# Planning an attention, Fourier-mix and MLP kernel with longer store and load latencies, and mirrored DFT tiles placed behind the last direct one

## The chip, the cores and the metric

The kernel runs on one core of one Trainium2 chip. The metric is device time in microseconds; for the kernel before it is 289.15 us, the median of 3 runs (288.5 to 289.49). The profile that is read below is one execution of it, with a span of 287.8 us from the first to the last instruction.

Short names used for the engines: PE is TensorE's matmuls, PEld its weight loads, DVE is VectorE, ACT is ScalarE, POOL is GpSimd, SP is the sync engine. SPq and POOLq are the instruction queues of SP and POOL, where DMA transfers are issued.

## The reference

Two computations follow each other, with 4 batches, 8 heads, 768 positions, 64 elements per head and a model width of 512:

```python
def _attn_ref(q, k, v, sort_net):
    ...
    P = sort_net                                   # 8 x 8 per head, five Sinkhorn steps
    ...
    k_sorted = np.einsum('bhij,bhjcd->bhicd', P, k_b)
    v_sorted = np.einsum('bhij,bhjcd->bhicd', P, v_b)
    scores = scale * np.matmul(q_b, k_sb.transpose(0, 1, 2, 4, 3))   # within blocks of 96
    ...                                            # softmax
    return np.matmul(attn, v_sb).reshape(B, H, S, D)

def _moe_ref(x, w_ch1, w_ch2):
    X = np.fft.fft(np.fft.fft(x, axis=1), axis=2)
    u = x + np.real(X)
    un = (u - mean(u)) / np.sqrt(var(u) + 1e-06)   # over the model width
    return u + np.maximum(un @ w_ch1, 0.0) @ w_ch2 # 512 -> 2048 -> 512
```

## The kernel before

**Work per batch.** For each of the 4 batches `b`, the kernel mixes keys and values with the Sinkhorn matrix (`kqt` L927 for keys, `v_mix` L742 for values, the latter fed by copies into `vcx` at L726), computes block scores (`scores`, L982), their exponentials on ACT (L991) with a correction by -1 (L1004 on DVE, L1006 on ACT), and the product with the values (`av`, L1021; then a reciprocal L1033 and a scaling L1036 on DVE). The result of a batch lies in a tile `rt`.

The Fourier mix has two stages. `dft1` transforms along the sequence: DVE folds `rt` (L1053 to L1137), PE multiplies (L1093 to L1103), ACT writes `y`. `dft2(b, g)` transforms along the model width. It works on 6 token tiles of 128 rows in two halves: `g = 0` has the tiles `T` = 0, 1, 2, `g = 1` has 3, 4, 5. Tiles 0, 1, 2 and 5 are direct: four matmuls of 256 columns with `y` (L1179) and one of 512 with the row terms `rb` (L1183), in a PSUM bank. Tiles 3 and 4 are mirrored: they reuse the banks of tiles 0 and 1, add one matmul (L1168), and are read backwards. For every tile DVE adds the residue into a buffer `u` (L1190 direct, L1202 and L1211 for `g = 1`), takes the statistics (L1216, L1218), and after ACT has computed the inverse deviation (L1222, L1225) the normalised rows `un` are written (L1242 on DVE, L1238 on ACT) and transposed into `ut` (by PE for batch 0, by SP's transposing DMA L1249 for the others).

`mlp(b, g)` takes `ut` of 384 tokens through both layers: 64 matmuls of the first layer (L1278, into banks of the group `pm`), 16 ReLU evictions into `hr` (L1290 on ACT, L1287 on DVE), 48 matmuls of the second layer (L1299), and per tile one DVE addition into `u` (L1307). Each tile of `u` is then stored: those of `g = 0` by SP as plain DMAs (L1312; the third tile in three pieces, L1314, L1316 and L1318, of 112, 15 and 1 rows), called the direct stores, and those of `g = 1` by POOL as an indirect DMA over a list of rows (L1322).

**Buffers that tie these together.** There are 6 buffers `u`, so `u` of `dft2(b+1, 0)` can only be written once the direct store of the same tile of batch `b` has landed. There are 5 PSUM banks in the group `pf` (scores, products, DFT) and 3 in `pm` (MLP). The transposed queries `qt` have 3 buffers. The keys and queries of batches 2 and 3 are loaded by POOL (`load_qk`, L500), and their transfers are held back by `after=lns[1:2]` until a certain normalisation of batch 0; these are the gated loads. Queries of batches 2 and 3 are transposed by SP (L945).

**The order.** A planner in the kernel (`Plan`) sets the order of all instructions before the program is built. Each operation is added with a pair of figures per engine, the time for which the engine is occupied and the time until the result can be used, and with a priority (`at(...)` sets it for a group, lower is sooner). `schedule` plays this forward: at each step the engine that is free first takes the operation of lowest priority figure that is ready, and buffers come free at the planned end of their last user. The planned times are used for nothing but the order; on the chip, each engine runs its list in that order and waits on semaphores for real. A planned figure that is too short thus places an instruction too early in its engine's list, and everything behind it on that engine then waits with it.

The change and the prediction's steps touch: `load` (L472, with `o.late` at L477), `dft2` (L1146, the mirrored branch L1164 to L1171, the direct one L1172 to L1187), the store in `mlp` (L1331), and the priorities of `dft2` at L1368, L1374 and L1377.

Of the kernel before, what the change touches and what calls it, by code (L numbers as in the profile page):

```python
# [348 lines left out]
def mm(n, k=1):  # L349
    return k * (n / 2400.0 + 0.004)  # L350


def pe(t):
    return {"PE": (t, t + 0.17)}
# [12 lines left out]
def kernel(  # L367
# [20 lines left out]
    P = Plan()  # L388
# [83 lines left out]
    def load(dst, src, nbytes, w, prio, eng="POOL", r=(), after=()):  # L472
        e = {"POOL": nc.gpsimd, "SP": nc.sync}[eng]
        c = (0.8, 0.8) if eng == "POOL" else (0.1, 2.3)
        o = P.add({eng: c}, lambda _: e.dma_start(dst, src), r=r, w=w,  # L475
                  prio=prio, nbytes=nbytes, tag="load", after=after)
        o.late = 4.0 if after else 0.0  # L477
        return o

    spin = Buf("pm")  # L480
# [1 line left out]
          tag="spin")  # L482
# [56 lines left out]
    for n in range(2):  # L539
# [10 lines left out]
          w=["smalls"], prio=-4996.6, tag="small")  # L550
# [53 lines left out]
    for it in range(5):  # L604
# [27 lines left out]
        r=["phi"], w=["pk"] + hk(1), tag="pk")  # L632
    P.add({"DVE": (0.14, 0.21)}, lambda _: V.tensor_tensor(
        phl[1], pw, phl[0], op=ALU.subtract), r=["pw", "phi"],
        w=["plo"] + hk(1), tag="pk", prio=P.prio + 20)
    for n, d_ in enumerate((pvh, pvl)):
# [5 lines left out]
              r=[("phi", "plo")[n]], w=[("pvh", "pvl")[n]] + hk(1), tag="pv",  # L642
# [8 lines left out]
    for hh in range(2):  # L651
        def f(_, hh=hh):
# [12 lines left out]
          r=[bk], w=["tkh"], prio=8.0, tag="tkh")  # L665
# [476 lines left out]
        chain(3)  # L1142

    banks_of = {}

    def dft2(b, g):  # L1146
        rt = rts[b]
# [3 lines left out]
        ym = [(y, c) for c in range(4)]  # L1151
        lts = [("rb", n) for n in range(4)] + [
            "rrow", "lt", "lt96", "lt96a", "lt96b", "lt96c", "dtab"]
        if g == 1:
            P.add({"DVE": (0.08, 0.16), "ACT": (0.18, 0.23)}, lambda e: copy(
                e, y.ap[:, :, 383:384], y.ap[:, :, 385:386]),
                r=ym, w=[(y, "z")] + ym, tag="yz")
        for tt in range(3):
            T = 3 * g + tt
            u, st = Buf("u"), Buf("st")  # L1160
            us[b, g].append(u)
            w0 = 128 * (T if T < 3 else 2)
            l0 = 128 * T if T < 3 else 384
            if T in (3, 4):  # L1164
                ps = banks_of[b, T - 3]

                def f(_, ps=ps, T=T):
                    nc.tensor.matmul(  # L1168
                        ps.ap, lt[:, LTD + 128 * (T - 3):LTD + 128 * (T - 2)],
                        rb, start=False, stop=True, skip_group_check=True)  # L1170
                P.add(pe(mm(512) + 0.03), f, r=lts, w=[ps, u], tag="dft2")  # L1171
            else:  # L1172
                ps = Buf("pf")
                banks_of[b, T] = ps

                def f(_, ps=ps, w0=w0, l0=l0):
                    for c in range(4):
                        o = 256 * (c % 2)
                        nc.tensor.matmul(  # L1179
                            ps.ap[:, o:o + 256], y.ap[:, c, w0:w0 + 128],  # L1180
                            dtab[:, c, :], start=(c == 0), stop=False,
                            skip_group_check=True)
                    nc.tensor.matmul(ps.ap, lt[:, l0:l0 + 128], rb,  # L1183
                                     start=False, stop=True,
                                     skip_group_check=True)
                P.add(pe(mm(256, 4) + mm(512) + 0.05), f,
                      r=ym + lts, w=[ps, u], tag="dft2")  # L1187
            if T < 3:
                P.add({"DVE": (0.6, 0.69)}, lambda _, u=u, ps=ps, T=T:
                      V.scalar_tensor_tensor(  # L1190
                          u.ap.rearrange("p (m n) -> p m n", n=2),
                          rt.ap[:, T, :].rearrange("p (m n) -> p m n", n=2),
                          RSC, ps.ap.rearrange("p (n m) -> p m n", n=2),
                          op0=ALU.mult, op1=ALU.add),
                      r=[ps] + [(rt, h) for h in range(H)], w=[u], tag="u")
            else:
                def f(_, u=u, ps=ps, T=T):
                    p_ = ps.ap
                    rev = bass.AP(
                        tensor=p_.tensor, offset=p_[:, 511:512].offset,  # L1200
                        ap=[p_.ap[0], [-1, 255], [-256, 2]])
                    V.scalar_tensor_tensor(  # L1202
                        u.ap[:, 1:511].rearrange("p (m n) -> p m n", n=2),
                        rt.ap[:, T, 1:511].rearrange(
                            "p (m n) -> p m n", n=2),
                        RSC, rev, op0=ALU.mult, op1=ALU.add)
                P.add({"DVE": (0.6, 0.69)}, f,
                      r=[ps] + [(rt, h) for h in range(H)], w=[u], tag="u")

                def f(_, u=u, ps=ps, T=T):  # L1210
                    V.scalar_tensor_tensor(  # L1211
                        u.ap[:, 0:512:511], rt.ap[:, T, 0:512:511], RSC,
                        ps.ap[:, 0:512:256], op0=ALU.mult, op1=ALU.add)
                P.add({"DVE": (0.1, 0.18)}, f,
                      r=[ps] + [(rt, h) for h in range(H)], w=[u], tag="u")
            P.add({"DVE": (0.6, 0.69)}, lambda _, u=u, st=st: V.bn_stats(  # L1216
                st.ap, u.ap), r=[u], w=[st], tag="bn")
            P.add({"DVE": (0.1, 0.17)}, lambda _, tt=tt, st=st: V.bn_aggr(  # L1218
                mv.ap[:, tt, :], st.ap), r=[st], w=[(mv, tt)], tag="bna")
# [4 lines left out]
            w=[(ny, 0)], tag="ln")  # L1224
# [4 lines left out]
            r=mvs + [ny], w=[nm], tag="ln")  # L1229
# [3 lines left out]
        for tt in range(3):  # L1233
            un, pt, u = Buf("un"), Buf("pf"), us[b, g][tt]

            def f(e, tt=tt, un=un, u=u):
# [4 lines left out]
                else:  # L1241
# [4 lines left out]
                  r=[u, ny, nm] + mvs, w=[un], tag="un")  # L1246
            if b > 0:
# [3 lines left out]
                      r=[un], w=[(ut, tt, 1)], tag="uX")  # L1251
                continue

            def f(_, un=un, pt=pt):
                p16 = pt.ap.bitcast(F16)
                for c in range(4):
# [10 lines left out]
                  r=[pt], w=[(ut, tt, 1)], tag="utev")  # L1267
# [3 lines left out]
    def mlp(b, g, pr_pe, pr_v):  # L1271
        ut = uts[b, g]
        for fc in range(16):
            ps = Buf("pm")

            def f(_, fc=fc, ps=ps):
                for c in range(4):
# [5 lines left out]
                  tag="ff1")  # L1283

            def f(e, fc=fc, ps=ps):
# [3 lines left out]
                else:  # L1289
# [3 lines left out]
                  w=[("h", g, fc)], prio=pr_v, tag="relu")  # L1293
        for tt in range(3):
            ps, u = Buf("pm"), us[b, g][tt]
            for qd in range(4):
                def f(_, qd=qd, tt=tt, ps=ps):
                    for fc in range(4 * qd, 4 * qd + 4):
# [4 lines left out]
                      r=[("w2", qd)] + [  # L1303
                          ("h", g, fc) for fc in range(4 * qd, 4 * qd + 4)],
                      w=[ps], prio=pr_pe + 0.1, tag="ff2")
# [3 lines left out]
            def f(_, u=u, T=3 * g + tt):  # L1309
# [16 lines left out]
                for x in st_:  # L1326
# [1 line left out]
                        tc.declare_no_dep(x.ins, y.ins,   # L1328
                                          reason="each row stored once")
                (stores if T > 2 else direct).extend(st_)  # L1330
            P.add({"SP": (0.1, 2.3)} if g == 0 else {"POOL": (1.2, 3.5)}, f,  # L1331
                  r=[(u, 1), "rows"], w=[], prio=pr_v, tag="out")


# [11 lines left out]
    def at(p, *fns):  # L1346
        for fn, a in fns:
            P.prio = p
            fn(*a)
# [15 lines left out]
    for hf in range(2):  # L1365
        load_qk("k", 2, hf, 62.0 + hf)
        load_qk("q", 2, hf, 62.5 + hf)
    at(20.0, (dft1, (1,)), (dft2, (1, 0)), (dft2, (1, 1)))  # L1368
    at(14.0, (a_path, (1,)), (a_rows, (2,)))
    at(30.0, (make_bdk, (2,)), (attn, (2,)))  # L1370
    for hf in range(2):
        load_qk("k", 3, hf, 64.0 + hf)
        load_qk("q", 3, hf, 64.5 + hf)
    at(40.0, (dft1, (2,)), (dft2, (2, 0)), (dft2, (2, 1)))  # L1374
    at(35.0, (a_rows, (3,)))
    at(50.0, (make_bdk, (3,)), (attn, (3,)))
    at(55.0, (dft1, (3,)), (dft2, (3, 0)), (dft2, (3, 1)))  # L1377
    for b in range(B):
        for g in range(2):
            mlp(b, g, 100.0 + 10 * (2 * b + (g if b < B - 1 else 1 - g)),  # L1380
# [43 lines left out]
```

## Time and profile before

| stretch, us | what runs mostly | PE busy, us | DVE busy, us | granted PE clock |
|---|---|---|---|---|
| 20 to 40 | attention of batch 0 | 18.90 of 20 | 18.97 | 1.00 |
| 40 to 60 | attention of batch 1, first Fourier mix | 18.60 of 20 | 19.71 | 1.00 |
| 60 to 80 | end of attention 1, MLP (0, 0) begins | 19.14 of 20 | 19.92 | 1.00 |
| 80 to 100 | values for batches 2 and 3, MLP (0, 0) | 19.50 of 20 | 19.43 | 1.00 |
| 100 to 120 | dft2 (1, 0), attention of batch 2, MLP (0, 1) | 16.03 of 20 | 13.90 | 0.91 |
| 120 to 280 | the rest, mostly MLP | 159.86 of 160 | 66.39 | 1.00 |

How to read it: busy time is the share in which an engine executes an instruction of the program; [...]. The stores and loads that the change speaks of take, from issue to landing: plain direct stores of 256 KB 2.0 us in the median and 4.1 us at most, the 15-row pieces 1.9, 4.7 and 7.5 us (smallest, median, largest), the indirect stores 2.7 us in the median, the gated loads that still run after 60 us between 4.9 and 9.8 us.

### The profile page before, as it was taken

How to read it: one execution, taken by the hardware profiler on the slowest of the kernel's cores; microseconds unless marked ns; L12 is line 12 of the kernel's file. 1: busy time of each engine (PE TensorE's matmuls, PEld its weight loads, DVE VectorE, ACT ScalarE, POOL GpSimd, SP SyncE). 2: the span in 40 equal slices, each digit the busy share in tenths (PEclk: the TensorE clock that was granted, in tenths of full speed). 3: DMA queues.
4: the chain of work that ended last, by engine and by line, in shares of the span. 5: the costliest groups of instructions: out<-in, count | busy, mean ns of one | idle time of the engine just before them, and what ended most of it. 6: DMA issues, size and time to landing. Idle time of an engine off the chain costs nothing.

```text
span 287.8 us, 5930 instructions
## 1 busy us (share of the span) xinstructions
PE 270.7 (94%) x2355; PEld 157.0 (55%) x2355; DVE 172.1 (60%) x424; ACT 158.0 (55%) x332; POOL 55.0 (19%) x81
## 2 busy tenths in 40 slices
PE   5999998999999986999999999999999999999991
PEld 2558876555745553554567456445545545545540
DVE  4599999999999974773489654136214415410010
ACT  2589889759689343885378126416704614614600
POOL 8993304150000280001300000021000012000022
PEclk9999999999999999799999999999999999999998
DMA  7999999999010299222102011211121012022002
GB/s 113 218 257 245 214 208 211 220 185 160 9 24 7 44 182 134 60 53 64 69 19 57 0 75 38 56 75 46 41 92 39 20 35 109 21 61 77 10 17 92
DMA packets 42529, 26.33 MB, mean 91 GB/s; under 512 B 30106, under 2 KB 38824, under 8 KB 42500
## 3 DMA queue, kind: packets, MB, share of 16 engines
q0 software_dynamic: 23536, 18.31, 37.7%
q1 hardware_dynamic: 18966, 7.64, 12.1%
q8 instruction: 18, 0.29, 0.4%
q14 instruction: 9, 0.07, 0.1%
HBM read 28.96 MB, written 6.29 MB: 122 GB/s over the span
## 4 chain that ended last, share of the span: by engine, by line
issue 49%; PE 26%; DVE 15%; POOL 4%; DMA 3%; ACT 0%; POOLq 0%; SPq 0%; DVEq 0%
PE bank L1299 5%; PE bank L1278 5%; PE bank L1391 4%; POOL out_dram L1322 4%; DMA out_dram<-u 3%; PE bank L742 2%; DVE rt L1036 2%; PE bank L927 2%; DVE st L1216 1%; PE bank L982 1%; PE bank L745 1%; DVE eb L1004 1%; PE bank L1093 1%; DVE hr L1287 1%; DVE pmt L1053 1%
## 5 line engine op out<-in xcount | busy, mean ns | idle before, releaser
L1290 ACT ACTIVATE hr<-bank 128x384 f16<-128x384 f32 x106 | 52.0, 491 | 81.9 <-PE bank L1278 75.6
L1278 PE MATMUL bank<-ut,w1sb 128*128 128x384 f16 x512 | 94.3, 329 | 0.7 <-DVE hr L1287 0.4
L1299 PE MATMUL bank<-w2sb,hr 128*128 128x512 f16 x384 | 88.5, 379 | 0.0
L1278 PEld LDWEIGHTS <-w1sb 128*128 128x128 f16 x512 | 48.5, 98 | 34.8 <-issue 2.1
L1299 PEld LDWEIGHTS <-hr 128*128 128x128 f16 x384 | 36.7, 98 | 41.3
L1307 DVE TENSOR_TENSOR u<-bank,u 128x512 f32<-128x512 f32 x24 | 16.5, 689 | 58.5 <-PE bank L1299 58.5
L1322 POOL DMA_INDIRECT out_dram<-u,rows x12 | 11.7, 971 | 164.3 <-DVE u L1307 137.5
L991 ACT ACTIVATE ex<-bank 96x384 f32<-96x384 f32 x64 | 28.1, 484 | 1.6 <-PE bank L982 1.2
L1391 PE MATMUL bank<-pack 128*128 128x480 f16 x63 | 18.0, 419 | 3.3 <-DMA pack<-k_pack 3.3
L1190 DVE SCALAR_TENSOR_TENSOR u<-rt,bank 128x512 f32<-128x512 f16 x12 | 8.1, 684 | 18.6 <-PE bank L1183 13.6
L1202 DVE SCALAR_TENSOR_TENSOR u<-rt,bank 128x510 f32<-128x510 f16 x12 | 8.1, 676 | 18.5 <-PE bank L1168 9.5
L1021 PEld LDWEIGHTS <-eb 97*128 97x128 f16 x416 | 15.8, 98 | 4.1 <-issue 1.8
L1006 ACT ACTIVATE eb<-ex,negone 96x384 f16<-96x384 f32 x30 | 17.9, 615 | 0.2
L1021 PE MATMUL bank<-vsf,eb 97*128 97x65 f16 x416 | 16.9, 193 | 0.9 <-DVE un L815 0.4
L475 POOL DMA_DIRECT2D kq<-in_k_dram x8 | 8.0, 995 | 50.5 <-DVE vcx L726 33.9
L1036 DVE TENSOR_TENSOR rt<-bank,rz 128x384 f16<-128x384 f32 x32 | 17.2, 546 | 0.3
L475 POOL DMA_DIRECT2D kq<-in_q_dram x20 | 16.3, 833 | 2.8 <-DVE rz L1033 1.3
L678 ACT CAST vsf<-bank 96x512 f16<-96x512 f32 x19 | 13.9, 793 | 4.6 <-PE bank L742 4.5
L1216 DVE BATCH_NORM_STATS2 st<-u 128x6 f32<-128x512 f32 x24 | 16.1, 685 | 0.3
L982 PE MATMUL bank<-qt,ks 64*128 64x96 f16 x256 | 11.7, 207 | 2.9 <-DVE u L1190 2.5
L1287 DVE TENSOR_SCALAR hr<-bank 128x384 f16<-128x384 f32 x22 | 12.1, 548 | 2.5 <-PE bank L1278 2.3
L1238 ACT ACTIVATE un<-u,nm,ny 128x512 f16<-128x512 f32 x14 | 11.3, 808 | 3.5 <-DMA ut<-un 1.8
(131 smaller groups left out, 330.3 us busy)
## 6 DMA issues: line engine op xcount, KB each, us to landing
kq<-in_k_dram POOLq DMA_DIRECT2D x8, 384.0 KB, 12.5
w1sb<-in_moe_w_ch_dram POOLq DMA_DIRECT2D x4, 512.0 KB, 16.7
w2sb<-in_moe_w_ch_dram POOLq DMA_DIRECT2D x4, 512.0 KB, 19.5
out_dram<-u SPq DMA_DIRECT2D x8, 256.0 KB, 2.0
kq<-in_q_dram POOLq DMA_DIRECT2D x4, 384.0 KB, 8.1
hr<-in_v_dram POOLq DMA_DIRECT2D x2, 768.0 KB, 12.4
kq<-in_v_dram POOLq DMA_DIRECT2D x2, 768.0 KB, 21.2
kq<-in_q_dram POOLq DMA_DIRECT2D x16, 96.0 KB, 8.2
```

Source lines behind the costliest of these rows:

```text
L475: o = P.add({eng: c}, lambda _: e.dma_start(dst, src), r=r, w=w, prio=prio, nbytes=nbytes, tag="load", after=after)
L991: nc.scalar.activation(ex.ap, pss[h2].ap[0:96, 0:384], AF.Exp, scale=SCALE),
L1006: nc.scalar.activation(ed, src, AF.Identity, bias=negone[0:96])
L1021: nc.tensor.matmul(po.ap[:, 65 * T:65 * T + 65], eb.ap[:, e0:e0 + 128], vsf[:, vi:vi + 65], start=(n == 0), stop=(n == len(WIN[T]) - 1), s ...
L1036: P.add({"DVE": (0.45, 0.56)}, lambda _: V.tensor_tensor(rt.ap[:, :, D * h:D * h + D], po3()[:, :, 0:D], rz.ap[:, :, None].broadcast_to([1 ...
L1216: P.add({"DVE": (0.6, 0.69)}, lambda _, u=u, st=st: V.bn_stats(st.ap, u.ap), r=[u], w=[st], tag="bn")
L1278: nc.tensor.matmul(ps.ap[:, 0:GT], w1sb[:, c, 128 * fc:128 * fc + 128], ut.ap[:, c, :], start=(c == 0), stop=(c == 3))
L1290: nc.scalar.activation(hr[g][:, fc, :], ps.ap[:, 0:GT], AF.Relu)
L1299: nc.tensor.matmul(ps.ap, hr[g][:, fc, 128 * tt:128 * tt + 128], w2sb[:, fc, :], start=(fc == 0), stop=(fc == 15))
L1307: V.tensor_tensor(u.ap, ps.ap, u.ap, op=ALU.add),
L1322: st_ = [nc.gpsimd.indirect_dma_start(out.rearrange("b s m -> (b s) m"), bass.IndirectOffsetOnAxis(ap=rows[:, i:i + 1], axis=0), u.ap, None)]
L1391: nc.tensor.matmul(spin.ap[:, 0:480], idh, pack.bitcast(F16))
```

## The change

It changes what the planner assumes and two orders that it is given; no part of the computation is added or removed. One more warm-up matmul (L1391) is issued, 64 for 63, and some operations that either engine can do change hands between DVE and ACT: four ReLUs, two of the corrections by -1 and one PSUM copy go to ACT, two normalisations to DVE.

- The planned latency of a gated load grows from 4.0 to 6.0 us on top of the transfer.
- The planned latency of a direct store grows from 2.3 us to 7.0 us for batches 0 to 2 and to 2.6 us for batch 3. In the plan, a buffer `u` of `g = 0` is therefore free later, and the DVE instruction that writes it next is placed later in DVE's list.
- The mirrored tiles 3 and 4 are planned only behind the last direct tile of `g = 0` (an order for PE, not a dependency of data).
- For batches 1 to 3, `dft2(b, 1)` gets a priority figure that is 0.5 higher than that of `dft2(b, 0)`, so that it follows it.

```diff
-        o.late = 4.0 if after else 0.0
+        o.late = 6.0 if after else 0.0
...
     banks_of = {}
+    d2last = []
...
-                P.add(pe(mm(512) + 0.03), f, r=lts, w=[ps, u], tag="dft2")
+                P.add(pe(mm(512) + 0.03), f, r=lts, w=[ps, u], tag="dft2",
+                      after=[d2last[-1]])
...
-                P.add(pe(mm(256, 4) + mm(512) + 0.05), f,
-                      r=ym + lts, w=[ps, u], tag="dft2")
+                d2last.append(P.add(
+                    pe(mm(256, 4) + mm(512) + 0.05), f,
+                    r=ym + lts, w=[ps, u], tag="dft2"))
...
-            P.add({"SP": (0.1, 2.3)} if g == 0 else {"POOL": (1.2, 3.5)}, f,
+            P.add({"SP": (0.1, 7.0 if b < 3 else 2.6)} if g == 0 else {"POOL": (1.2, 3.5)}, f,
...
-    at(20.0, (dft1, (1,)), (dft2, (1, 0)), (dft2, (1, 1)))
+    at(20.0, (dft1, (1,)), (dft2, (1, 0)))
+    at(20.5, (dft2, (1, 1)))
...
-    at(40.0, (dft1, (2,)), (dft2, (2, 0)), (dft2, (2, 1)))
+    at(40.0, (dft1, (2,)), (dft2, (2, 0)))
+    at(40.5, (dft2, (2, 1)))
...
-    at(55.0, (dft1, (3,)), (dft2, (3, 0)), (dft2, (3, 1)))
+    at(55.0, (dft1, (3,)), (dft2, (3, 0)))
+    at(55.5, (dft2, (3, 1)))
```

## The prediction

> **What bounds the kernel now.** I read the busy line of the page first, then PE's busy time and clock by stretches of the span, then what PE waited for, and last the timelines around the one stretch that stood out.
>
> ```profile
> PE 270.7 (94%) x2355; PEld 157.0 (55%) x2355; DVE 172.1 (60%) x424; ACT 158.0 (55%) x332; POOL 55.0 (19%) x81
> ...
> 70.00:100.00 30.00, 29.36 (x284) 17.41 (x283) 29.35 (x58) 21.28 (x47) 1.33 (x2) 1.00 0.16 30
> 100.00:120.00 20.00, 16.03 (x177) 9.93 (x176) 13.90 (x35) 9.62 (x22) 6.87 (x10) 0.91 1.25 132
> 120.00:282.00 162.00, 161.86 (x1092) 87.56 (x1088) 66.39 (x154) 73.52 (x160) 11.95 (x22) 1.00 0.18 50
> ```
>
> PE is the bound. The columns after the length of a stretch are PE, PEld, DVE, ACT, POOL, then the granted clock. From 120 us to the last matmul PE has no gap (161.86 of 162), so every microsecond won or lost before 120 us reaches the end. Between 100 and 120 us PE idles 4.0 us and the clock falls to 0.91. The stretch in slices of 2 us shows where:
>
> ```profile
> 112.00:114.00 2.00, 0.55 (x10) 0.40 (x10) 1.28 (x3) 0.00 (x0) 0.00 (x0) 1.00 1.34 104
> 114.00:116.00 2.00, 1.57 (x8) 0.61 (x6) 2.00 (x6) 0.95 (x4) 0.00 (x0) 0.66 0.64 105
> 116.00:118.00 2.00, 2.00 (x14) 0.88 (x13) 1.58 (x5) 1.68 (x6) 0.00 (x0) 0.50 0.05 11
> ```
>
> PE stands still and then works at half clock for a while. The next fence puts together lines of PE's timeline (three), DVE's (one), and the chain of waits (one); each has start, length, and what.
>
> ```profile
> 107.85 0.60 PE L1179 MATMUL bank<-vcx,y 128*128 128x256 f16 x4 [1.09 <-DVE rt L1036]
> 113.45 0.35 PE L982 MATMUL bank<-qt,ks 64*128 64x96 f16 x8 [2.45 <-DVE u L1190]
> 114.98 1.44 PE L1278 MATMUL bank<-ut,w1sb 128*128 128x384 f16 x4 [0.43 <-DVE hr L1287]
> ...
> 112.72 0.69 DVE L1190 SCALAR_TENSOR_TENSOR u<-rt,bank 128x512 f32<-128x512 f16 x1 [3.69 <-DMA out_dram<-u]
> ...
> 104.99 7.54 DMA out_dram<-u
> ```
>
> The 15-row piece of the third direct store of batch 0 is issued at 104.99 and takes 7.54 us. The write of that buffer for dft2 (1, 0), tile 2, is next in DVE's list at 109.0 and waits 3.69 us. Its PSUM bank stays taken and the ReLUs behind it wait, so PE lacks banks for scores (2.45 us) and MLP (0.43 us). Lost on PE: 1.09 + 2.45 + 0.43 = 3.97 us. Lost to the clock: 2.00 x (1 - 0.66) + 2.00 x (1 - 0.50) + 2.00 x (1 - 0.98, the slice from 118 us) = 1.72 us. Together 5.7 us.
>
> [...] 1.72 us lost is 3.4 us at one half. [...] no gap here is longer than 2.45 us. [...] POOL issues ten gated loads from 98.17 to 106.7 us, and the 15-row piece takes 7.54 us in their midst against 1.9 us at best. [...]
>
> **The change part by part.** I compared the order of the instructions on each engine before and after, and laid the durations of the rows of before end to end along both lists (DVE: L1190, L1216 and L1307 0.60 each, L726 1.40, L1036 0.46, L1287 0.47; PE: L1278 0.1625 and L1299 0.2165 per matmul), with no waits.
>
> *Longer latency of direct stores.* It is what reorders the stretch from 76 to 134 us. Between the addition that completes the stored buffer (L1307) and DVE's next write of it (L1190), DVE has this much other work, before and after: tile 0, 3.5 and 7.0 us; tile 1, 2.6 and 6.5; tile 2, 3.5 and 8.0. Needed is the landing plus the way to the issue: 2.0 to 4.1 us for tiles 0 and 1, and for tile 2 8.0 us (L1307 ends at 104.49, the store lands at 112.53). Tiles 0 and 1 are covered; tile 2 just so. The gated loads wait for the last L726 copy, which by the sums ends about 1.5 us earlier than before, at 97.2 to 98, while the third store comes at about 105 to 106 us, so it meets the same loads: between 6 and 7.5 us. The work moved in front is batch 2's attention and first DFT fold, which had stood behind. So the 3.97 us go, and with them the cause of the 1.72 us: **-5.7 us**. Kept for the range: 0 to 2 us of the wait stay.
>
> *What the new order costs.* DVE is at 29.35 of 30 us in the 70 to 100 stretch, and the new order pulls deadlines together. Before, the last two L726 copies ended at 99.02 and the values' last matmuls (L742) began at 100.19, 1.2 us of slack; after, the sums bring both to 97.2, no slack, and head 0's L1021 follows with 1.5 us of MLP between instead of 2.4. The same holds for the group before it, at 90.5 to 90.8. I take 0.7 us. From 101 us on, scores, exponentials and products of batch 2 run closer behind each other; PE and DVE meet within 0.5 us at each of 8 heads. I take another 0.5 us. **+1.2 us**; the small waits of before in these places (8.36 us more on the clock from 76 to 134 us than the sum of PE's work, 5.7 of them named above) give a scale, 2.7 us, so the range is 0 to 3.
>
> *Latency of gated loads, 4 to 6 us.* It moves the first use of batch 3's keys and queries relative to their issue. Keys of the first half are complete about 5 us after issue by the packets (98.2 to about 103), and their first use in the new order is at about 110: hidden, 0. Behind SP's direct stores now stand four query transposes in place of two before the first normalised rows (L1249), the last of which must wait for a buffer `qt` that PE frees at about 118. Behind it wait the three transposes of (1, 0), and for these the first-layer matmuls of (1, 0). I put their landing at about 127, and PE gets there at about 134 (139.1 before, less the gain): hidden, 0.
>
> *Mirrored tiles behind the last direct one, and priority +0.5.* For batch 0 one L1168 of 0.22 us changes places with eight score matmuls, with DVE's list the same and DVE the tighter engine (19.71 of 20 us): 0. The extra warm-up matmul fills a gap: 0. For batches 2 and 3 the L1168 stand behind 48 second-layer matmuls, not 40 to 44. The distance from the last direct tile's L1183 to the first L1278 that needs the result is 28 x 0.1625 + 40 x 0.2165 = 13.2 us before and 40 x 0.1625 + 32 x 0.2165 = 13.4 after for batch 3, and before the last transpose was issued at 252.9 for a use at 259.38: hidden, 0.
>
> *The end.* Before, PE ends at 282.03, the last tile's addition at 282.83, POOL's store is issued at 283.11 and lands 2.7 us later, 3.8 after PE; the span ends 2.0 us after that. After, the last tile is a direct one: addition to +0.80, the 1-row piece issued 0.87 us after the first (265.57 - 264.70), landing in 2.0: +3.7. POOL's last tile is done four matmuls (0.87 us) sooner: +2.9. **-0.1 us**, at most -0.9.
>
> Sum: 289.15 - 5.7 + 1.2 - 0.1 = 284.55, rounded to **284.5 us**.
>
> **The rivals.** (a) *The wait returns in another place:* the third store lands later than DVE comes to it, or L742 waits for the copies by 2 to 3 us. For it: no slack in two places. Against it: ACT and the PSUM groups leave PE some MLP to do. With half of the 5.7 us back: about 287.3. (b) *DVE sets the pace from 60 to 118 us,* so that taking out one wait only spreads it over others and PE starves as long as before. For it: DVE at 19.92 and 19.43 of 20 us. Against it: in 100 to 120 us DVE is busy for 13.90 only, and four ReLUs go to ACT. Gain under 0.6: about 288.9. (c) *Slower:* the (1, 0) transposes, now behind two more query transposes on SP (6.6 us in the median from issue to landing, 8.8 in this stretch), land at about 139 instead of 127; PE runs out of MLP work at 134, idles 5 us and loses 1.7 us of clock again: 284.5 + 6.7 = 291.2. For it: the SP list is strictly in order. Against it: 12 us of lateness would have to come together.
>
> **How the numbers follow.** The forecast has 0.62, (a) 0.20, (b) 0.08, (c) 0.10. The forecast's own bounds: all small waits gone too, 289.15 - 8.4 - 0.9 = 279.9, which I give no weight; no new wait and the full tail 282.6; 3 us of new waits 286.4. To leave out about (b) and (c) and no more, the range takes in (a) and runs from 282.7 to 287.7. Within 0.3% means 288.28 to 290.02. Faster: forecast and (a), 0.82; same: (b), 0.08; slower: (c), 0.10.
>
> **What will show it.** In the profile after: PE's gap on L982 or L1278 behind "DVE u L1190" gone, the clock at 1.00 in 100 to 120 us and PE busy above 18.5 of 20 there; DVE's wait for out_dram<-u under 1.5 us; PE gaps at L742 or L1021 of up to 1 us in 90 to 102; no PE gap at the first L1278 of (1, 0) near 134; the last store a direct one. The forecast is wrong if PE shows a gap of over 2 us anywhere from 76 to 140, or a second stretch at half clock.

## The result, and the profile after

The changed kernel takes 284.56 us (median of 4 runs, 284.15 to 284.76) against 289.32 us for the kernel before in the same session (4 runs, 288.5 to 289.8): a ratio of 0.9837, 95% interval 0.9811 to 0.9862, 1.6% less. In a second session it took 285.07 us (6 runs) against 288.6, ratio 0.9872 (0.9848 to 0.9897). The forecast was 284.5 us.

The kernel before does not repeat to better than about 1%, in part because PE's clock falls in about half of its runs (67 of the 137 of the experiments; in the profile that was read, to 0.50 from 114.65 to 118.07 us) and not in the others, and the medians below have both in them.

In the changed file the lines from L1168 on have moved: the direct tile's write into `u` is now L1193 (before L1190), the MLP's matmuls are L1281 and L1302 (L1278, L1299), the ReLU on DVE L1290 (L1287), the addition L1310 (L1307), the direct stores L1315 to L1321 (L1312 to L1318), the indirect store L1325 (L1322). The busy line of the page after:

```profile
PE 269.0 (95%) x2356; PEld 156.7 (55%) x2356; DVE 169.7 (60%) x419; ACT 160.7 (57%) x337; POOL 55.0 (19%) x81
```

The stretches after, in the columns of the prediction's fence (length, then busy time of PE, PEld, DVE, ACT, POOL, granted clock, DMA share, GB/s), and the three slices around the old gap:

```profile
70.00:100.00 30.00, 29.16 (x293) 18.00 (x291) 29.50 (x57) 22.88 (x51) 2.90 (x4) 1.00 0.23 36
100.00:120.00 20.00, 20.00 (x262) 12.72 (x260) 17.65 (x45) 15.00 (x35) 5.38 (x8) 1.00 1.12 126
...
112.00:114.00 2.00, 2.00 (x43) 1.40 (x39) 1.92 (x6) 1.07 (x3) 0.00 (x0) 1.00 0.81 160
114.00:116.00 2.00, 2.00 (x23) 1.14 (x18) 1.98 (x5) 1.80 (x5) 0.00 (x0) 1.00 0.35 67
116.00:118.00 2.00, 2.00 (x20) 1.10 (x18) 2.00 (x6) 1.03 (x3) 0.00 (x0) 1.00 0.01 4
```

PE is still the bound, with 95% for 94%. The stretch from 100 to 120 us holds 20.00 us of PE work in 20.00, where it held 16.03, and the clock is 1.00 in it for 0.91. The three slices around the old gap are full. What is worse stands in the line above: 70 to 100 us has 29.16 for 29.36.

PE's waits of over 0.2 us after 60 us, from its timeline after:

```profile
80.32 0.84 PE L742 MATMUL bank<-bdv,vcx 128*128 128x128 f16 x12 [0.27 <-DVE vcx L726]
82.04 2.11 PE L1281 MATMUL bank<-ut,w1sb 128*128 128x384 f16 x12 [0.42 <-DVE vsf L678]
```

DVE's write of the third buffer, from its timeline after:

```profile
116.00 0.69 DVE L1193 SCALAR_TENSOR_TENSOR u<-rt,bank 128x512 f32<-128x512 f16 x1
```

The issue of the 15-row piece in SP's timeline after:

```profile
108.11 0.43 SPq L1319 DMA_DIRECT2D out_dram<-u  x1
```

And the landing of that one piece, from the answer on its line (L1319, 95 to 120 us):

```profile
DMA to landing us min/median/max: 4.1/4.1/4.1
```

PE's waits are 0.27 and 0.42 us; none is left at the scores. The write at 116.00 has no bracket: DVE did not wait. The piece is issued at 108.11 and lands 4.1 us later, at 112.2, so 3.8 us are in hand. Before it was issued at 104.99 and landed at 112.53.

The end of the timeline after:

```profile
277.55 0.96 POOL L1325 DMA_INDIRECT out_dram<-u,rows  x1 [4.58 <-DVE u L1310]
...
278.09 0.33 SPq L1317 DMA_DIRECT2D out_dram<-u  x1
278.47 0.43 SPq L1319 DMA_DIRECT2D out_dram<-u  x1
278.95 0.73 SPq L1321 DMA_DIRECT2D out_dram<-u  x1
```

The last tile is a direct one: SP issues its three pieces behind POOL's last store.

### The profile page after: what moved, and what is told of

The parts are those of the page before. It is cut to its first block, busy times and chain, and to the rows that moved or that the text cites. A ratio compares the mean times of both kernels' runs of the same rounds, so it can differ in the third digit from the quotient of the medians.

```text
span 283.0 us, 5927 instructions
## 1 busy us (share of the span) xinstructions
PE 269.0 (95%) x2356; PEld 156.7 (55%) x2356; DVE 169.7 (60%) x419; ACT 160.7 (57%) x337; POOL 55.0 (19%) x81
## 4 chain that ended last, share of the span: by engine, by line
issue 58%; PE 14%; DVE 13%; POOL 7%; DMA 5%; ACT 1%; POOLq 0%; DVEq 0%
DMA hr<-in_v_dram 5%; POOL out_dram L1325 4%; POOL kq L475 3%; PE bank L1281 2%; PE bank L1302 2%; PE bank L742 2%; DVE rt L1036 2%; PE bank L745 1%; DVE st L1219 1%; PE bank L1093 1%; DVE eb L1004 1%; PE bank L982 1%; DVE pmt L1053 1%; PE bank L927 1%; DVE bdk L669 1%
## 5 line engine op out<-in xcount | busy, mean ns | idle before, releaser
L1293 ACT ACTIVATE hr<-bank 128x384 f16<-128x384 f32 x110 | 54.0, 491 | 72.0 <-PE bank L1281 65.1
L1281 PE MATMUL bank<-ut,w1sb 128*128 128x384 f16 x512 | 91.5, 326 | 0.7 <-DVE vsf L678 0.4
L1302 PE MATMUL bank<-w2sb,hr 128*128 128x512 f16 x384 | 87.9, 379 | 0.0
L1281 PEld LDWEIGHTS <-w1sb 128*128 128x128 f16 x512 | 48.8, 98 | 33.9 <-issue 1.0
L1302 PEld LDWEIGHTS <-hr 128*128 128x128 f16 x384 | 36.4, 98 | 41.2
L1310 DVE TENSOR_TENSOR u<-bank,u 128x512 f32<-128x512 f32 x24 | 16.5, 689 | 67.9 <-PE bank L1302 67.8
L1325 POOL DMA_INDIRECT out_dram<-u,rows x12 | 11.7, 971 | 160.1 <-DVE u L1310 159.5
L1397 PE MATMUL bank<-pack 128*128 128x480 f16 x64 | 16.8, 395 | 3.3 <-DMA pack<-k_pack 3.3
L1006 ACT ACTIVATE eb<-ex,negone 96x384 f16<-96x384 f32 x32 | 19.0, 615 | 0.2
L1021 PEld LDWEIGHTS <-eb 97*128 97x128 f16 x416 | 15.8, 98 | 3.4 <-issue 1.1
L1021 PE MATMUL bank<-vsf,eb 97*128 97x65 f16 x416 | 17.1, 193 | 0.5 <-DVE un L815 0.2
L475 POOL DMA_DIRECT2D kq<-in_k_dram x8 | 6.4, 799 | 49.9 <-PE bank L927 48.9
L1193 DVE SCALAR_TENSOR_TENSOR u<-rt,bank 128x512 f32<-128x512 f16 x12 | 8.0, 682 | 11.2 <-PE bank L1185 11.2
L1205 DVE SCALAR_TENSOR_TENSOR u<-rt,bank 128x510 f32<-128x510 f16 x12 | 7.9, 677 | 10.1 <-PE bank L1169 6.4
L678 ACT CAST vsf<-bank 96x512 f16<-96x512 f32 x17 | 12.6, 789 | 2.0 <-PE bank L742 1.9
L1241 ACT ACTIVATE un<-u,nm,ny 128x512 f16<-128x512 f32 x12 | 9.7, 810 | 6.5 <-DMA ut<-un 4.4
L678 ACT CAST ks<-bank 128x384 f16<-128x384 f32 x23 | 10.7, 478 | 3.3 <-PE bank L927 3.2
L742 PE MATMUL bank<-bdv,vcx 128*128 128x128 f16 (+1 forms) x128 | 12.0, 220 | 0.3 <-DVE vcx L726 0.3
```

The lines of the kernel that those rows point to most:

```text
L678: (nc.scalar.copy if e == "ACT" else V.tensor_copy)(dst, src)
L742: nc.tensor.matmul(o, vcx[:, 96 * d:96 * d + m], bd, start=True, stop=(t == 1))
L1006: nc.scalar.activation(ed, src, AF.Identity, bias=negone[0:96])
L1021: nc.tensor.matmul(po.ap[:, 65 * T:65 * T + 65], eb.ap[:, e0:e0 + 128], vsf[:, vi:vi + 65], start=(n == 0), stop=(n == len(WIN[T]) - 1), s ...
L1281: nc.tensor.matmul(ps.ap[:, 0:GT], w1sb[:, c, 128 * fc:128 * fc + 128], ut.ap[:, c, :], start=(c == 0), stop=(c == 3))
L1293: nc.scalar.activation(hr[g][:, fc, :], ps.ap[:, 0:GT], AF.Relu)
```

## The experiments

Two theories stood at first. **W**: the wait of DVE for the third direct store of batch 0 is what the change removes, and the store's planned latency alone does most of it. **L**: the longer latency of the gated loads, or the order of the DFT tiles, carries a good part. Later ones are named where they come up. Each session had its own runs of the kernel before: medians 289.61 (43 runs), 289.2 (67) and 288.6 (27) for the three groups of four runs below, each group on another chip. The ratio, not the time, is what compares across sessions.

| run | what it is | median, us | ratio to before, 95% interval |
|---|---|---|---|
| e1_store_only | store's latency 7.0 alone | 285.62 | 0.9872 (0.981 to 0.9934) |
| e4_all_but_store | the change without it | 287.82 | 0.9947 (0.9922 to 0.9972) |
| e7_store_45 | the change, 4.5 for 7.0 | 285.40 | 0.9871 (0.9809 to 0.9933) |
| e5_fill_gap | before, filling behind the gap | 290.52 | 1.0056 (1.0033 to 1.0079) |
| e5b_fill_gap4 | before, filling in the gap | 288.43 | 0.998 (0.9959 to 1.0001) |
| e6_u8 | before, 8 buffers `u` | 290.33 | 1.0027 (0.9997 to 1.0058) |
| e3_dft_only | DFT order and priorities alone | 288.57 | 0.9997 (0.9973 to 1.0021) |
| e11_change_u8 | the change, 8 buffers `u` | 288.93 | 0.9981 (0.9956 to 1.0006) |
| e13_short_queries | before, less traffic beside the store | 286.44 | 0.9915 (0.9882 to 0.9948) |
| e10_change_again | the change | 285.07 | 0.9872 (0.9848 to 0.9897) |
| e9_store_10 | the change, 10.0 for 7.0 | 288.23 | 0.9975 (0.996 to 0.9991) |
| e12_load_8 | the change, loads 8.0 for 6.0 | 284.40 | 0.9857 (0.9831 to 0.9884) |

### Which part carries the gain

**e1_store_only**, the store's latency alone:

```diff
-            P.add({"SP": (0.1, 2.3)} if g == 0 else {"POOL": (1.2, 3.5)}, f,
+            P.add({"SP": (0.1, 7.0 if b < 3 else 2.6)} if g == 0 else {"POOL": (1.2, 3.5)}, f,
```

> The kernel before with one part of the change: planned latency of direct stores 7.0 us for batches 0 to 2 and 2.6 for batch 3. Between the addition into u (tile 2) and DVE's next write of it stand now 8.3 us of DVE work (3.5 before, 8.0 with the whole change). Theory W (the wait for the third direct store and what follows from it are the whole difference): no DVE wait for out_dram<-u over 1 us, PE busy over 19.5 of 20 us and clock 1.00 from 100 to 120 us, 284 to 285.5 us. Rival L (the longer latency of gated loads, which loosens the stretch from 76 to 100 us, carries half of the gain or more): 286.5 to 288 us.

**e4_all_but_store**, the other side: that line as before, all else as in the change.

> The whole change but for the direct stores, which are planned with 2.3 us as before: gated loads 6.0 us, mirrored tiles behind the last direct one, priorities +0.5. DVE work between the addition into u and its next write: tile 2 2.8 us (3.5 before), tile 1 3.2, tile 0 6.4. Theory W: DVE waits 3.5 to 5 us for the third store, PE stands still for 2 us or more around it, the clock falls again: 288.5 to 290.5 us. Rival L: 284.5 to 287 us.

**e7_store_45**, a smaller dose: the whole change with 4.5 in place of 7.0.

> The whole change, with the direct stores of batches 0 to 2 planned at 4.5 us in place of 7.0. DVE work between the addition into u and its next write: tile 2 5.8 us, tile 1 5.2, tile 0 6.4. Theory W, by its size: landing 6 to 8 us behind the addition less 5.8 us of work leaves a DVE wait of 0 to 2 us, PE idles less than 1.5 us and the clock holds: 284.5 to 286.5 us. Rival T (it takes the full latency; any wait on the third store stalls PE's banks and the clock): 287.5 to 289.5 us.

**e3_dft_only**: `d2last` and the priorities of the second DFT, with both latencies as before.

> Only the mirrored tiles behind the last direct one and the priorities of the second DFT; planned latencies of stores and loads as before. The order of DVE and ACT is that of the kernel before; on PE one mirrored matmul of batch 0 and a warm-up matmul stand elsewhere. All theories: within 0.3% of before, 288.7 to 290.4, with the third store's wait of 3 to 4 us and the low clock after it still there. If the mirrored tiles carried part of the gain, it would be 288 or less.

The stretch from 100 to 120 us (columns as above) in e1:

```profile
100.00:120.00 20.00, 19.59 (x255) 12.91 (x253) 17.97 (x46) 13.51 (x31) 7.55 (x10) 1.00 1.33 139
```

in e4:

```profile
100.00:120.00 20.00, 18.45 (x241) 11.38 (x240) 17.15 (x45) 11.91 (x28) 5.27 (x8) 1.00 1.21 133
```

in e7:

```profile
100.00:120.00 20.00, 19.82 (x257) 12.50 (x255) 18.83 (x48) 14.72 (x36) 5.16 (x8) 1.00 1.26 130
```

and in e3:

```profile
100.00:120.00 20.00, 17.00 (x216) 11.29 (x215) 15.01 (x38) 11.44 (x27) 6.65 (x10) 1.00 1.18 138
```

e1 has PE at 19.59 and e7 at 19.82, both with no wait of DVE on a store; e4 has 18.45 and e3 17.00. In time, e1 reaches a ratio of 0.9872, the same as the whole change in one session (0.9872) and a little short of it in the other (0.9837); a share of at most 1 us for the rest of the change beside it can't be told from the spread. Those ratios also depend on how often the clock fell in the runs of before. Against only those runs of before that kept it (288.48 us on the mean beside e1, 288.39 beside e10, the changed kernel's second session; how they are told apart stands under "What the clock is worth"), e1 gains 2.9 us and the whole change 3.4. The order of the DFT tiles and the priorities alone are nothing, 0.9997. So W holds, and 4.5 us was already enough.

e4 met neither expectation: it gains, 0.9947, less than L wanted and more than W. Its timeline of DVE says how:

```profile
105.45 0.69 DVE L1193 SCALAR_TENSOR_TENSOR u<-rt,bank 128x512 f32<-128x512 f16 x1 [2.28 <-DMA out_dram<-u]
```

as does the landing of the 15-row piece, from the answer on its line:

```profile
DMA to landing us min/median/max: 1.9/1.9/1.9
```

The longer planned loads changed the order around the stores too. The wait is now at the second store (2.28 us, where the kernel before has 0.66 there and 3.69 at the third), and the 15-row piece is issued at 111.02 instead of 104.99 and lands in 1.9 us. PE's gaps in the stretch are 0.99 and 0.56 us, where they were 3.97 in all. So the loads' latency, by another way, hits part of the same wait. The two parts are not additive, since there is one wait to remove: 1.28% and 0.53% against the 1.28 to 1.63% of the whole.

### What the clock is worth

**e5_fill_gap** was to keep PE at work in the gap of the kernel before with useless matmuls:

```diff
-                for c in range(4):
+                for c in list(range(4)) * (4 if (b, g, fc) == (0, 1, 6) else 1):
```

> The kernel before, where the four matmuls of first-layer block 6 of MLP (0, 1), the last PE work ahead of the 2.45 us gap, are issued four times in place of once (the same result, written again): 12 more matmuls of 0.1625 us, 1.95 us of PE work inside the gap, the order of everything else as before. It parts the clock's share from the wait's. Theory C (the gap itself drops the clock and costs 1.7 us on top of the idle time): the clock stays at 1.00 from 100 to 120 us, the DVE wait of 3 to 4 us stays, 287.2 to 288.2 us. Rival N (the clock falls for another reason, such as the PE idling shares around it, or the filling delays the ReLU behind it): the clock falls as before, 289.0 to 291 us.

It missed its aim: the filled block stood behind the gap, not in it, as PE's timeline shows, so its 290.52 us tell nothing of what the clock costs.

```profile
113.77 0.35 PE L982 MATMUL bank<-qt,ks 64*128 64x96 f16 x8 [1.75 <-DVE u L1190]
...
115.30 4.38 PE L1278 MATMUL bank<-ut,w1sb 128*128 128x384 f16 x16 [0.42 <-DVE hr L1287]
```

The gap is still there (1.75 us), and the 16 matmuls behind it take 4.38 us, 0.27 each for the 0.17 that they take at full clock (20 in 3.42 us in the timeline of the next run). **e5b_fill_gap4** has the same edit with column block 4.

> The kernel before, with the four first-layer matmuls of column block 4 of MLP (0, 1) issued four times: 12 more matmuls (12 x 0.1625 = 1.95 us of PE work) stand directly ahead of the gap of 2.45 us, on a bank that is free anyway; the result is unchanged. This time the filling is in front of the score matmul that waits, which it was not in the run with column block 6. Theory C (of the 5.7 us that the stretch loses, 1.7 are the clock, which falls because PE stands still): the filling costs nothing, DVE's wait for the third store stays near 3.7 us, the gap shrinks to about 0.5 us, the clock stays at 1.00 from 110 to 120 us, and the time falls by up to 1.7 us, to 287.6 to 288.8. Theory N (the clock falls for another reason, or the half clock is hidden behind other waits): clock below 0.95 in 100 to 120 us all the same, and 289.0 to 291.5.

PE's timeline in e5b:

```profile
109.17 3.42 PE L1278 MATMUL bank<-ut,w1sb 128*128 128x384 f16 x20
112.53 0.34 PE L982 MATMUL bank<-qt,ks 64*128 64x96 f16 x8
```

DVE's write of the third buffer in it:

```profile
111.77 0.69 DVE L1190 SCALAR_TENSOR_TENSOR u<-rt,bank 128x512 f32<-128x512 f16 x1 [3.10 <-DMA out_dram<-u]
```

and its slices of 2 us (columns as above):

```profile
114.00:116.00 2.00, 1.96 (x24) 1.17 (x24) 2.00 (x6) 1.89 (x6) 0.00 (x0) 1.00 1.23 78
116.00:118.00 2.00, 2.00 (x33) 1.43 (x30) 1.97 (x8) 1.79 (x4) 0.00 (x0) 1.00 0.23 47
```

20 matmuls run from 109.17 and the score matmul behind them has no wait, although DVE still waits 3.10 us for the store. The clock stays at 1.00 in the slices that had 0.66 and 0.50. And it seems to do so in every run. The mean granted clock over the span tells the runs apart: the kernel before has runs at 0.988 to 0.991 and runs at 0.993 to 0.999, and none between (the mean also holds the half clock behind PE's last matmul, 0.50 from 285.3 us to the end in the trace of before, so a single run near the line can be misplaced). Of the 22 of the filled kernel, none is below 0.9925, against 35 of 67 of the kernel before beside it. Those 35 average 290.10 us, the other 32 average 288.32, 1.78 us apart; in the other two sessions the two groups are 1.64 and 1.45 us apart. So the fall of the clock costs about the 1.72 us that the prediction read from one profile, but only in about half of the runs: some 0.9 us on the mean. The filled kernel's mean, 288.53, is 0.72 below that of the 67 runs and 0.2 above the group with the high clock. The interval of the ratio (0.9959 to 1.0001) just touches 1, so the count of runs is the firm part of this finding.

### Removing the wait by other means

**e6_u8** gives the kernel before two more buffers `u`, in a table that is dead by then:

```diff
+    tabf = tab.rearrange("p a b w -> p (a b w)")
+    P.pools["u"] += [(90.0, 6 + i, tabf[:, 512 * i:512 * i + 512])
+                     for i in range(2)]
```

> The kernel before, all planned latencies as before, with two more buffers u (8 for 6) laid into a table that nothing reads any more after the Sinkhorn steps. Nothing has to wait for a direct store to land then, in the plan or on the chip. Theory W (the wait for the store is what the change takes away; longer planned latency is one way to do it): no wait of DVE for out_dram<-u, PE above 18.5 of 20 in 100 to 120 us at clock 1.00, 284.0 to 286.5. Theory O (the change gains by the order that it gives the engines elsewhere, and the wait only happens to go too): the wait is gone here as well, but the gain is less than half, 287.0 to 290.

Its lines stand 3 further down than before's (L985 is L982, the scores; L1205 and L1214 are L1202 and L1211, a mirrored tile's writes into `u`). DVE's timeline in e6:

```profile
112.99 0.69 DVE L1205 SCALAR_TENSOR_TENSOR u<-rt,bank 128x510 f32<-128x510 f16 x1 [4.34 <-DMA out_dram<-u]
```

PE's:

```profile
114.26 0.50 PE L985 MATMUL bank<-qt,ks 64*128 64x96 f16 x8 [3.69 <-DVE u L1214]
```

and the slices from 116 and 118 us (columns as above):

```profile
116.00:118.00 2.00, 2.00 (x34) 1.74 (x33) 1.94 (x7) 1.74 (x4) 0.00 (x0) 0.50 0.74 87
118.00:120.00 2.00, 2.00 (x18) 0.90 (x18) 1.67 (x6) 1.00 (x3) 0.00 (x0) 0.50 0.73 140
```

Both theories had said that the wait would be gone, and it was not. The planner used the new buffers for tiles 0 and 1 of (1, 0) and then put the mirrored tiles of (1, 1) forward into what they left free: the third store's buffer was wanted as soon as before, by another tile. DVE waits 4.34 us at L1205 for the same piece, which takes 7.2 us to land, PE waits 3.69, the clock halves at about 113.5 us and is still at 0.50 in the slice up to 120, over 6 us where before has 3.4, and the time is no better than that of before. The run does not separate W from its rival O (e13 below does), but it shows that the wait costs no less when another tile meets it, and that more buffers don't help where the plan believes that a store takes 2.3 us.

**e11_change_u8** has the same two buffers in the changed kernel (its L1248, L1284 and L1293 are L1242, L1278 and L1287 of before).

> The whole change and two more buffers u besides. Theory W: with the change no store is waited for any more, so two more buffers have nothing left to take away: 284.0 to 285.3, as the change alone. Rival D (the longer latency in the plan has a price, because it pushes DVE work about, and a plan without that constraint is better): 282.5 to 283.9, and the sum of the small PE waits between 76 and 120 us is lower than with the change alone.

DVE's timeline in e11:

```profile
115.33 0.55 DVE L1248 TENSOR_SCALAR un<-u,mv,ny 128x512 f16<-128x512 f32 x1 [3.48 <-DMA ut<-un]
```

and PE's:

```profile
116.39 1.44 PE L1284 MATMUL bank<-ut,w1sb 128*128 128x384 f16 x4 [2.67 <-DVE hr L1293]
```

It met neither range: 288.93. The mirrored tiles are early here as well, so DVE comes early to writing `un`, and waits 3.48 us until SP's transposes have read its two buffers; ReLUs stand behind it, and PE idles 2.67 us. This is another resource with the same kind of wait, so the run tells nothing of rival D. It is near to the prediction's rival (c), which feared for the transposes on SP's list.

### Why the store lands late

**e13_short_queries** keeps the order of every instruction of the kernel before and takes away traffic beside the store:

```diff
-                    :, h // 2, h % 2],
-                    src[b, 4 * hf + h].rearrange("(r p) d -> p r d", r=6),
+                    :, h // 2, h % 2, 0:6 if b == 2 else 1],
+                    src[b, 4 * hf + h].rearrange("(r p) d -> p r d", r=6)[:, 0:6 if b == 2 else 1],
```

> The kernel before with the order of every instruction as it is; only the eight query loads of batch 3, which are in flight beside the third store, move one of six rows per position group (16 KB instead of 96 KB each). Five sixths of batch 3's queries are thus left out, and what lies in their place is multiplied instead. Theory R (the 15-row piece of the third store lands late because the gated loads share the DMA engines with it): it lands in 2 to 3.5 us after its issue instead of 7.5, DVE's wait falls below 0.5 us, PE's gap of 2.45 us and the half clock go, the gap of 1.1 us on L1179, which lies before the third store, stays: 289.2 - 2.9 - 0.9 (half of the runs with 1.7 us of low clock) = 285.4, range 284.6 to 286.5. Rival S (the small piece is slow by itself, or because of what is ahead of it on its own queue): it still takes 5 to 7.5 us, and the time is 288.3 to 290.

DVE's timeline in e13:

```profile
111.16 0.69 DVE L1190 SCALAR_TENSOR_TENSOR u<-rt,bank 128x512 f32<-128x512 f16 x1 [2.16 <-PE bank L1278]
```

PE's:

```profile
111.91 0.34 PE L982 MATMUL bank<-qt,ks 64*128 64x96 f16 x8 [0.92 <-DVE u L1190]
```

the landing of the 15-row piece, from the answer on its line:

```profile
DMA to landing us min/median/max: 5.3/5.3/5.3
```

and the packets of POOL's queue (q0) from 108 to 110 us, with their number, MB, and summed time as the page's share:

```profile
q0 software_dynamic: 196, 0.05, 25.3%
```

The same row of the kernel before:

```profile
q0 software_dynamic: 1175, 0.22, 134.0%
```

R was right in direction and wrong in size. The piece, issued at 105.69, lands in 5.3 us instead of 7.54, which is still within the 5 to 7.5 of S; PE's gap shrinks from 2.45 to 0.92, and the time is 286.44, at the upper edge of R's range and far from that of S. The clock stays up in all 4 runs, which would happen by luck about one time in six, as 17 of 27 runs of before beside it kept it. The gap on L1179, which R had expected to stay, shrinks from 1.09 to 0.38: DVE's wait of 0.66 us for the second store is gone as well. Note how DVE's line is to be read: the profile puts the 2.16 us down to a matmul of the MLP, but this instruction reads another bank, complete at 108.65; what came at 105.69 + 5.3 = 110.99 is the store.

The run also does what e6 could not. With the order of every instruction unchanged and the waits shorter, PE's two gaps lose 0.71 + 1.53 = 2.24 us, and the mean of its runs, 286.49, is 1.9 below the 288.39 of those runs of before that kept their clock. So the wait itself costs about what PE's gaps show, and theory O is not needed for that part.

The key loads and the rest of the queries were left in, and POOL's queue was not empty until about 110 us. So the gated loads are a cause of the late landing; whether all of it is theirs, and whether their bytes or their time of issue count, this run leaves open, since with fewer bytes POOL was also done issuing them sooner (105.42 us, 0.3 ahead of the piece; in the kernel before 1.8 behind it). In ten other profiles, that of before among them, the landing follows the time from POOL's last gated load to the piece: issued before that load is out or up to 0.6 us behind it (before, e1, e3, e5b, e7), the piece lands in 5.7 to 7.5 us; issued 2.0 to 2.9 us behind it (the change, e10, e9), in 4.1 to 4.3; 4.9 and 5.9 us behind it (e12, e4), in 1.9.

### How much latency to plan

**e10_change_again** is the changed kernel, as a measure for the two that follow.

> The changed kernel once more, as a measure for the others on this chip: 284.2 to 285.0, no run below a mean clock of 0.9925, while about half of the runs of before are.

It took 285.07, the top of that range and a little over, and its clock was high in 6 of 6 runs, where 10 of 27 of the kernel before were low. **e9_store_10** has 10.0 where the change has 7.0:

> The whole change with 10.0 us for the planned latency of the direct stores in place of 7.0. DVE has 8.9, 9.6 and 10.3 us of other work between a buffer's addition and its next write. Theory W (the latency only has to be long enough to cover the landing): nothing more to gain, and what it pushes back costs at most a little, 284.2 to 285.8. Rival M (more is better, since the store just barely landed in time): under 284.0. Rival P (pushing DVE's writes back has a price on PE's banks): above 286.

Rival P: 288.23, 3.2 us above the change beside it. PE's timeline has what the change's has up to 120 us, and then this:

```profile
188.23 1.46 PE L1281 MATMUL bank<-ut,w1sb 128*128 128x384 f16 x8 [0.70 <-DMA ut<-un]
195.28 0.50 PE L1093 MATMUL bank<-cs,fq 128*128 128x386 f16 x2 [1.29 <-DVE fq L1137]
...
237.53 1.46 PE L1281 MATMUL bank<-ut,w1sb 128*128 128x384 f16 x8 [0.42 <-DVE u L1310]
243.51 6.01 PE L1281 MATMUL bank<-ut,w1sb 128*128 128x384 f16 x36 [0.61 <-DVE hr L1290]
```

0.70 + 1.29 + 0.42 + 0.61 = 3.02 us of new gaps, late in the span, where PE had no gap to lose. The figure holds for the stores of batches 1 and 2 as well, and I read the gaps as what it does there: DVE work that others need is put off for a landing that was no danger. That reading was not tested further.

**e12_load_8** has 8.0 us of extra latency for the gated loads instead of 6.0:

> The whole change with 8.0 us for the planned extra latency of the gated loads in place of 6.0; the store's stays at 7.0. Theory W (the loads' latency matters only through where it puts the third store among the loads, and DVE's list keeps 6 us or more between the buffers' uses): no wait on the store, 284.2 to 285.8. Rival L (the second knob carries gain of its own, as the run with the longer loads and the short store let suppose, and 6.0 is not yet its end): under 284.0.

The landing of the 15-row piece in e12, issued at 107.51 us:

```profile
DMA to landing us min/median/max: 1.9/1.9/1.9
```

and the packets of SP's queue (q1) from 108 to 110 us:

```profile
q1 hardware_dynamic: 452, 0.32, 58.8%
```

The loads start at 94.03 us for 96.25 in e10, POOL's queue q0 has no row left between 108 and 110, and the piece, issued 0.2 us sooner than in e10 and with the same stores ahead of it in SP's queue, lands in 1.9 us for 4.1. That speaks against rival S. The time is 284.40 (284.04 to 285.18) against 285.07 (284.44 to 285.2): as W expected. The means of six runs each are 0.43 us apart and their ranges overlap, so that it is better than the change is not shown.

## Why the prediction held

- **What bounds it, and where the 5.7 us lie.** Right. PE's 3.97 us of gaps were real: e1, e7, e10 and e12, which lack them, end at 284.4 to 285.6. The clock's 1.72 us was right for a run in which the clock falls and too large for the mean: it falls in 67 of the 137 runs of before in the three sessions. The term is worth about 0.9, and the 5.7 should have been about 4.9. The profile that was read was of a run with a low clock, and one profile could not tell. The 3.97 may be large for a mean run too: e3, with the latencies of before, has 1.09 + 1.49 + 0.42 = 3.00 us in the same places in its profile.
- **Longer latency of direct stores: the wait goes.** Right in effect (no wait of DVE; gap gone; e1 and e7 confirm the cause). Off in detail: the piece was to be issued at 105 to 106 us, land in 6 to 7.5, and be "just covered". e1, which has this edit alone, did that: issued at 105.79, landed in 6.6. In the whole change it was issued at 108.11 and landed in 4.1, with 3.8 us in hand.
- **What the new order costs, +1.2.** Too dear, and put down to the wrong edit. Of the 0.7 for L742 and L1021 from 90 to 102 us and the 0.5 from 101 us on, nothing came: PE has no wait of 0.2 us or more there. Two new waits stand earlier, 0.27 at L742 (80.32) and 0.42 at an L1281 behind `vsf` (82.04). e4, without the store's edit, has both, and e1 and e3 have neither, so they come with the latency of the gated loads. Two of 0.3 us each in the kernel before (L1021 behind `u` L1211, L1093 behind `fq`) went, so 0.1 net. The scale was mis-sized: durations laid end to end gave 8.36 us beyond PE's work from 76 to 134 us, 2.7 of them small waits. The trace of before has PE busy for 53.53 of these 58 us, so idle for 4.47, of which 3.97 are the named gaps: 0.5 us of small waits.
- **Luck.** The two misses hid each other. 5.7 - 1.2 + 0.1 = 4.6 was forecast; 4.9 - 0.1 + 0.1 = 4.9 would have been the better sum, and about 4.5 for the second session, in which the clock fell in only 10 runs of 27. Measured were 4.8 (first session) and 4.0 (means of the second). So the cause was foreseen, but that the time was met within 0.1 us is luck, and the half microsecond that the second session lacks is not explained beyond the doubt on the 3.97.
- **Latency of gated loads: 0.** Wrong as a statement on this edit alone: e4 gains 0.53% with it (e3, without it, nothing), by moving stores and loads past each other. Beside the longer store latency its share is at most about 1 us and not separable. The step looked only at the first uses of the loaded rows, and neither at the traffic beside the store nor at what the new order does near 80 us.
- **Mirrored tiles and priorities: 0.** Right: e3, 0.9997.
- **The end: -0.1.** Right: the last store is a direct one, and the span ends 5.65 us after PE's last matmul (at 277.34) in place of 5.77.
- **Rivals.** (a) The wait did not return in the change; a wait on a store did in e4 and e6 and one on a transpose in e11, each with another instruction in the queue, so it was the right thing to fear. (b) DVE does not set the pace from 100 to 120 us: PE has 20.00 of 20 with DVE at 17.65. (c) PE has no gap near 134 us; the four transposes on SP's list were in time.
- **What was to show it.** Gap gone, clock 1.00 and PE at 20.00 of 20, no DVE wait on the store, no gap near 134, a direct store last: these signs are there. The waits of up to 1 us at L742 or L1021 from 90 to 102 us are not; the 0.27 us at L742 lies at 80.

## What to carry to other kernels

Where a planner orders the instructions, look at real landings in the place where each buffer is reused, not at the median: the stores' median of 2.0 us was good enough for most of them, and the one that met the loads cost PE nearly 3 us (2.45 and 0.43) and, in 67 of 137 runs, the clock. Plan enough to cover that landing and no more (4.5 and 7.0 did, 10.0 put other operands late), and expect that extra buffers alone will be used up by a plan that still believes in the short latency. Before a clock loss seen in one profile goes into a sum, count in how many runs it happens.

## What was new about the hardware

**When the clock fell.** In the trace of the kernel before, the granted clock is 1.00 from 8.84 us, where its record begins, except from 114.65 to 118.07 us and from 285.32 on, behind PE's last matmul, where it is 0.50. The stretch ahead of the first fall, as long as the half clock, and the half clock itself (columns as above):

```profile
111.24:114.65 3.41, 1.10 (x12) 0.60 (x12) 1.94 (x4) 0.36 (x1) 0.00 (x0) 1.00 1.46 81
114.65:118.07 3.42, 3.09 (x17) 1.31 (x17) 2.93 (x9) 2.70 (x8) 0.00 (x0) 0.50 0.34 66
```

Slices of e3, in whose profile the clock did not fall:

```profile
110.00:112.00 2.00, 0.77 (x5) 0.34 (x4) 0.49 (x1) 1.36 (x3) 0.00 (x0) 1.00 1.75 161
112.00:114.00 2.00, 1.32 (x14) 0.75 (x14) 2.00 (x6) 0.15 (x1) 0.00 (x0) 1.00 0.90 71
114.00:116.00 2.00, 2.00 (x30) 1.28 (x29) 2.00 (x7) 1.79 (x7) 0.00 (x0) 1.00 0.47 94
```

PE did some work in the 3.41 us ahead of each fall between 113 and 116 us: 1.10 us in the kernel before, 1.33 in e5, 0.48 in e6 and 1.39 in e11, where slices of 2 us put the fall at about 115.2, 113.5 and 115.8 us. In e3 it was busy for 1.93 us from 109.49 to 112.91, around its gap of 1.49 us, and the clock stayed at 1.00. The half clock lasted 3.4 us in the kernel before and in e5; in e6 and e11 it still held at 120 us, over 6 and over 4 us after the fall. PE was busy for 3.09 of its first 3.42 us in the kernel before, for 2.66 in e6 and for 2.77 in e11. The changes of the clock in the trace of before lie 105.81, 3.41 and 167.25 us apart from the start of its record on, 31, 1 and 49 times 3.41 us; in the trace of the changed kernel the one change comes after 273.07 us, 80 times. What sets the fall and its length is not shown by so few cases.

**Why it looks like chance.** With the same kernel, 67 of 137 runs have a low mean clock; 12 more matmuls (1.95 us) in the gap of 2.45 us leave none of 22. e3 has it in 8 of 22 and e4 in 9 of 20, with profiles of runs that kept the clock; the gaps of their other runs are not recorded. The changed kernel and e1, e7, e9 and e12, with no such gap in this stretch, have it in none of 46 runs. With one trace for each kernel, what parts the runs is not shown.

**A small store beside loads.** A store of 15 rows took between 1.9 and 7.5 us to land. The orders of these kernels differ in more than this, but what the time goes with is how long after the last of ten loads in another queue the store is issued: 1.9 us when 4.9 us or more behind it, 5.7 and more when at most 0.6 us behind it or ahead of it. It was 5.3 us when most of the bytes of eight of these loads were left out.
